# First batch's scan with two components in slices of four, VectorE's order written out

## Chip, core and metric

The kernel runs on one core of a Trainium2 chip. The core has TensorE (PE; its weight loads are listed as PEld), VectorE (DVE), ScalarE (ACT), GpSimd (POOL) and SyncE, whose queue (SPq) issues the DMAs. The metric is device time in microseconds, the median of several runs.

## What is computed

The inputs are q, k, v and a complex decay a = a_re + i a_im, each of 4 batches, 8 heads, 768 tokens and 48 channels. The part that matters here is the attention with a state:

```
mag = np.sqrt(a_re * a_re + a_im * a_im)
scale = np.minimum(mag, 0.999) / (mag + 1e-06)
a_re_n, a_im_n = (a_re * scale, a_im * scale)
for t in range(S):
    ar, ai = (a_re_n[:, :, t, :, None], a_im_n[:, :, t, :, None])
    new_re = ar * S_re - ai * S_im
    new_im = ar * S_im + ai * S_re
    kv = np.einsum('bhd,bhe->bhde', k[:, :, t], v[:, :, t])
    S_re, S_im = (new_re + kv, new_im)
    y[:, :, t] = np.einsum('bhd,bhde->bhe', q[:, :, t], S_re)
```

Then follow, for each batch, a two-dimensional Fourier transform (real part, added to its input), a normalisation, an MLP (384 to 1536 to 384), a token mixer (768 to 256 to 768) and a second MLP, each added to its input.

## The kernel before

Each batch's 768 tokens are cut into 8 chunks of 96. In a chunk the decays up to a token multiply up to a running product P, so q is multiplied by P and k is divided by it, and the attention inside a chunk is an ordinary masked product. P is a scan of 49 sequential steps for all chunks and heads at once: 128 partitions (64 pairs of head and chunk, run backwards and forwards from the middle of the chunk), 48 channels, on VectorE. Its result lies in PSUM (tiles `p`).

`stage1(b)` does this for batch b. Before the change, every batch uses the same code, in slices of three steps (`SL`, 16 slices and a last one of a single step):

- `st_a` loads the decays (`raw`) and q, k (`xx`) of a slice. For batch 0, slices 4 to 15 are loaded in large pieces of 12 steps (line 332), the first slices one by one (337, 343).
- `st_b`, `st_c`, `st_d`, `st_e` turn raw decays into factors: squares on ScalarE (351), their sum on GpSimd (356), logarithm, clamp and exponential on ScalarE (362 to 364), a Newton step (365, 366, 372 to 374) and the limit at 0.999 (382, 383). `A` then holds five rows for each step: the real part twice or as needed (384, 385), the imaginary part with both signs (386, 388) and, in row 2, the squared inverse magnitude (387).
- `st_f` is one step: 410 multiplies the three components of P (real, imaginary, and the squared inverse magnitude R) by rows 0 to 2 of `A`, 413 forms the cross products, 414 adds them. Line 407 caps R once in a slice.
- `st_g` multiplies q and k by P: 423 gives the first product, 424 multiplies the other operand by R (which turns a product with P into a division), 426 gives the second, and 427 and 428 store both in HBM (`kn`).
- `st_t` transposes them on TensorE (445) and ScalarE copies the result to `qkt` (448, 450, 451).
- `st_end` compares R times the squared length of P with 1 in the last step; `good` becomes `gate`, and a gate of zero in any batch makes a slow exact loop run at the end of the kernel (`fallback`).

After the scan, `ch_load` reads the stored products back for each chunk (`Kn`, 502), `ch_sc` forms scores (511, 518) and `ch_u`, `ch_y` carry the state from chunk to chunk (526 to 568). Beside that, `tick` and `convert` turn the 64-bit weights into pairs of 32-bit ones (181 to 203) in the background. From there on the MLPs of one batch run on TensorE while the next batch's scan runs on VectorE; for batch 0 there is no earlier batch, and the scan runs alone.

A scheduler sets the order of each engine's instructions from the program's order, priorities (`RANK`) and its own estimate of durations; each engine then runs its queue in order and waits on semaphores. `warm` adds matmuls whose result is not used (305), in batch 0 two of them from slice 10 on.

## Time and profile before

| | us |
|---|---|
| median of 3 runs | 1112.63 (1111.71, 1112.63, 1117.65) |
| the profiled execution | 1115.16 |
| its span, first to last instruction | 1113.4 |
| busy in the span: PE, DVE, ACT, POOL | 991.1, 795.6, 517.8, 372.7 |

The profiled execution is 1.8 us longer than its span, and 2.53 us above the median. The shares of busy time are averages over stages with different limits: the first batch's scan, where TensorE has little to do, its chunks with the conversion of the weights beside them, and the long stage in which TensorE multiplies.

### The profile page before, as it was taken

What the parts mean: (1) busy time and instruction counts of PE and PEld (TensorE: products, weight loads), DVE (VectorE), ACT (ScalarE), POOL (GpSimd) and SP (SyncE); (2) the same over time, 40 slices, a digit from 0 to 9 for tenths busy, and PEclk for the clock granted to TensorE, in tenths of its full rate; (3) what the DMA queues carried; (4) which work ended last, traced back from release to release, by engine and by line L of the source; (5) the groups of instructions that cost most, each with busy time, mean ns of one, the idle gap of its engine ahead of it and who ended that gap; (6) DMA issues with size and microseconds to landing.
All of it is one profiled execution on the core that took longest, in us unless ns stands there. A gap on an engine that the chain in (4) does not pass through costs nothing.

```text
span 1113.4 us, 21166 instructions
## 1 busy us (share of the span) xinstructions
PE 991.1 (89%) x7322; PEld 924.0 (83%) x7322; DVE 795.6 (71%) x2161; ACT 517.8 (47%) x1442; POOL 372.7 (33%) x510
## 2 busy tenths in 40 slices
...
GB/s 215 41 38 137 255 265 142 177 273 235 199 190 242 213 170 190 56 202 148 175 199 184 102 99 190 191 171 149 122 79 43 158 127 115 170 142 135 163 100 74
DMA packets 102466, 174.67 MB, mean 157 GB/s; under 512 B 11216, under 2 KB 63568, under 8 KB 101840
## 3 DMA queue, kind: packets, MB, share of 16 engines
...
q14 instruction: 54, 0.44, 0.1%
...
## 4 chain that ended last, share of the span: by engine, by line
PE 64%; DVE 8%; DMA 3%; ACT 1%; POOL 1%; issue 1%; SPq 0%; POOLq 0%; DVEq 0%; ACTq 0%
PE l L744 23%; PE l L728 22%; PE s L511 3%; PE s L445 2%; DMA cvt<-wL 2%; PE s L835 2%; PE s L560 2%; PE s L824 1%; PE s L566 1%; PE s L949 1%; DVE ws L784 1%; DVE ws L790 1%; PE s L526 1%; PE s L967 1%; PE s L708 1%
## 5 line engine op out<-in xcount | busy, mean ns | idle before, releaser
L744 PE MATMUL l<-w,h 128*128 128x384 f32 x1728 | 331.0, 344 | 12.8 <-DVE h L734 8.8
L728 PE MATMUL l<-th,w 128*128 128x384 f32 x1152 | 313.8, 342 | 5.3 <-DVE h L734 2.6
L744 PEld LDWEIGHTS l<-w,h 128*128 128x128 f32 x1728 | 302.8, 191 | 17.8 <-DVE h L734 12.4
L728 PEld LDWEIGHTS l<-th,w 128*128 128x128 f32 x1152 | 210.3, 189 | 9.4 <-DVE h L734 4.4
L732 ACT ACTIVATE h<-l 128x384 fp32r<-128x384 f32 x192 | 94.1, 490 | 226.0 <-PE l L728 225.2
L728 PE MATMUL l<-tl,w 128*128 128x384 f32 x576 | 194.8, 338 | 0.0
L734 DVE SCALAR_TENSOR_TENSOR h<-l,h 128x384 fp32r<-128x384 f32 x192 | 106.1, 552 | 87.9 <-ACT h L732 87.4
L747 DVE TENSOR_TENSOR u<-u,l 128x384 f32<-128x384 f32 x192 | 105.4, 550 | 76.5 <-PE l L744 75.4
L445 PE MATMUL s<-misc,y 128*112 128x128 f32 x384 | 71.0, 306 | 60.0 <-DVE y L423 38.3
L445 PEld LDWEIGHTS s<-misc,y 128*112 128x112 f32 x384 | 50.2, 148 | 77.1 <-POOL A L384 17.6
L728 PEld LDWEIGHTS l<-tl,w 128*128 128x128 f32 x576 | 108.8, 189 | 0.7 <-DVE tl L712 0.5
L192 POOL TENSOR_TENSOR cvt<-cvt 128x384 int32<-128x384 int32 x56 | 64.4, 1156 | 37.5 <-ACT sq L351 8.1
L366 POOL TENSOR_TENSOR tm<-tm 128x144 f32<-128x144 f32 (+1 forms) x68 | 35.3, 519 | 101.1 <-ACT tm L365 100.9
L511 PE MATMUL s<-qkt 112*96 112x96 f32 x512 | 59.9, 267 | 7.4 <-DVE sc L518 6.7
L511 PEld LDWEIGHTS s<-qkt 112*96 112x96 f32 x512 | 53.6, 177 | 10.6 <-DVE sc L518 7.5
L410 DVE TENSOR_TENSOR p<-p,A 128x144 f32<-128x144 f32 x192 | 59.5, 310 | 3.0
L202 POOL TENSOR_TENSOR w<-cvt,w 128x384 fp32r<-128x384 f32 x44 | 52.6, 1204 | 8.9 <-ACT w L201 8.7
L544 POOL TENSOR_TENSOR yc<-Aa,gm 48x384 f32<-48x384 f32 x18 | 21.0, 1165 | 101.4 <-DVE Aa L537 101.4
L384 POOL TENSOR_TENSOR A<-raw,tm 128x144 f32<-128x144 f32 (+1 forms) x68 | 34.9, 513 | 59.2 <-DVE tm L382 33.2
L195 DVE SCALAR_TENSOR_TENSOR cvt<-cvt 128x384 int32<-128x384 int32 x56 | 46.8, 843 | 8.7 <-POOL cvt L192 8.5
L414 DVE TENSOR_TENSOR p<-p,yt 128x96 f32<-128x96 f32 x192 | 50.1, 261 | 3.5
L934 POOL TENSOR_TENSOR xl<-u,xh 128x384 fp32r<-128x384 f32 x18 | 18.0, 1009 | 101.1 <-ACT xh L933 101.1
(182 smaller groups left out, 1805.1 us busy)
## 6 DMA issues: line engine op xcount, KB each, us to landing
...
kn<-y SPq DMA_DIRECT2D x128, 96.0 KB, 2.1
Kn<-kn SPq DMA_DIRECT2D x64, 192.0 KB, 3.9
...
```

The source lines that it names most:

```text
L192: x = ge.tensor_tensor(out=a, in0=a, in1=lo, op=ALU.add)
L195: rest(ve.scalar_tensor_tensor(out=a, in0=hi, scalar=-0x80000000, in1=a, op0=ALU.bitwise_and, op1=ALU.bitwise_or))
L202: ge.tensor_tensor(out=parts[:, 1, :], in0=a.bitcast(F32), in1=r32(parts[:, 0, :]), op=ALU.subtract)
L410: x = ve.tensor_tensor(out=cur, in0=prev, in1=A[:, j, 0:3, :], op=ALU.mult)
L414: ve.tensor_tensor(out=cur[:, 0:2, :], in0=cur[:, 0:2, :], in1=y, op=ALU.add)
L445: te.transpose(ps[:, j, :], y[:, j, 0:112], ident)
L511: te.matmul(out=ps[:, j, :], lhsT=K[:, hc, :], rhs=Q[:, hc, :])
L728: te.matmul(out=ps, lhsT=w1[:, wi, kt * 128:kt * 128 + 128], rhs=x[g][:, kt, :], start=(n == 0), stop=(n == 8))
L732: x = se.activation(out=hi, in_=ps, func=ACTF.Relu)
L734: ve.scalar_tensor_tensor(out=h[:, 1, g * 384:g * 384 + 384], in0=ps, scalar=0.0, in1=r32(hi), op0=ALU.max, op1=ALU.subtract)
L744: te.matmul(out=ps, lhsT=hs[m][:, hi, tt * 128:tt * 128 + 128], rhs=w2[:, wi, :], start=(n == 0), stop=(n == 8))
L747: ve.tensor_tensor(out=u[tt], in0=u[tt], in1=ps, op=ALU.add)
```

## The change

Batch 0 gets a scan of its own, `first_scan`; the other batches run the code as it was, now under the name `scan`. In `first_scan`:

- A slice has four steps (`SL4`, 12 slices and the last step); the two pieces of P (real and imaginary) are all that the scan carries. `A` has three rows. The clamp (363) and the second factor (374, 383, 387) are gone, and so is the cap (407).
- The inverse squared length is formed for a whole slice after its four steps (`st_s`): squares on ScalarE out of PSUM (430), sum on GpSimd (432), logarithm and exponential on ScalarE (433, 434), a product on GpSimd (435), and a Newton step on VectorE (`st_r`, 450). `st_x` (455) multiplies it into `xx`; `st_y` (444) gives the two products, `kn` is stored from 446.
- VectorE's instructions are chained by hand with `vq`: each one's place behind the one before is fixed. `line_up(i)` says which instructions of other slices stand between the three of a step. ScalarE also sums 1/|a|^2 into `low` (373), which the check at the end reads.
- All loads are issued ahead (slices 0, 1, 2 one by one, then three large pieces). `warm` starts at slice 8 of 12, two matmuls of 512 columns instead of 384.

```
-W0, WS, W1, W3 = 2, 10, 0, 0
+N4 = 4
+SL4 = [(N4 * i, N4) for i in range(12)] + [(48, 1)]
+W0, WS = 2, 8
-    ybuf = [[pool.tile([128, NT, 128], F32, name=f"y{k}{j}") for j in range(2)] for k in range(2)]
+    ybuf = [[pool.tile([128, N4, 128], F32, name=f"y{k}{j}") for j in range(2)] for k in range(2)]
...
+        def vq(x):
+            if last[0] is not None:
+                after(x, last[0])
+            last[0] = x
+            return x
...
+        def st_c(i):
+            tm = t[i]["tm"]
+            x, r0, tt = (tm[:, j, :] for j in range(3))
+            se.activation(out=r0, in_=x, func=ACTF.Ln, bias=tiny)
+            se.activation(out=r0, in_=r0, func=ACTF.Exp, scale=-0.5)
+            se.activation(out=tt, in_=r0, func=ACTF.Square, accum_out=low[:, i:i + 1])
+            ge.tensor_tensor(out=tt, in0=x, in1=tt, op=ALU.mult)
+        def st_d(i):
+            tm = t[i]["tm"]
+            r, tt = tm[:, 1, :], tm[:, 2, :]
+            vq(ve.scalar_tensor_tensor(out=r, in0=tt, scalar=-3.0, in1=r, op0=ALU.add, op1=ALU.mult))
+            se.activation(out=tt, in_=r, func=ACTF.Copy, scale=-0.25e-6 * ACL, bias=-0.5 * ACL)
+        def st_e1(i):
...
+            vq(ve.scalar_tensor_tensor(out=c1, in0=r, scalar=-2.0 / ACL, in1=tt, op0=ALU.max, op1=ALU.mult))
+            ge.tensor_tensor(out=A[:, :, 0, :], in0=raw[:, :, 0, :], in1=c1, op=ALU.mult)
+        def st_e2(i):
...
+            vq(ve.scalar_tensor_tensor(out=A[:, :, 2, :], in0=raw[:, :, 1, :], scalar=sgn, in1=d["c1"], op0=ALU.mult, op1=ALU.mult))
+            ge.tensor_scalar(out=A[:, :, 1, :], in0=A[:, :, 2, :], scalar1=-1.0, scalar2=None, op0=ALU.mult)
+            P = palloc("l" if i % 3 == 2 else "p", [128, N4, 96])
...
+            x = vq(ve.tensor_tensor(out=cur, in0=prev, in1=A[:, j, 0:1, :].to_broadcast([128, 2, 48]), op=ALU.mult))
+            marked(x)
+            d.setdefault("scan", x)
+            vq(ve.tensor_tensor(out=y, in0=prev[:, 1::-1, :], in1=A[:, j, 1:3, :], op=ALU.mult))
+            for f in between[0:1]:
+                f()
+            vq(ve.tensor_tensor(out=cur, in0=cur, in1=y, op=ALU.add))
+            for f in between[1:]:
+                f()
+        def st_s(i):
...
+            se.activation(out=e, in_=d["P"], func=ACTF.Square)
+            x, r = e[:, :, 0, :], e[:, :, 1, :]
+            ge.tensor_tensor(out=x, in0=x, in1=r, op=ALU.add)
+            se.activation(out=r, in_=x, func=ACTF.Ln, bias=wee)
+            se.activation(out=r, in_=r, func=ACTF.Exp, scale=-1.0)
+            ge.tensor_tensor(out=x, in0=x, in1=r, op=ALU.mult)
+        def st_y(i, k):
...
+            vq(ve.tensor_tensor(out=o, in0=x, in1=d["P"], op=ALU.mult))
+            h = slice(64 * k, 64 * k + 64)
+            sp.dma_start(out=knd[k, :, s0:s0 + m, :], in_=y[h, 0:m, :])
+        def st_r(i):
+            e = t[i]["ss"]
+            vq(ve.scalar_tensor_tensor(out=e[:, :, 0, :], in0=e[:, :, 0, :], scalar=-2.0, in1=e[:, :, 1, :], op0=ALU.add, op1=ALU.mult))
+        def st_x(i):
...
+            vq(ve.scalar_tensor_tensor(out=x, in0=d["ss"][:, :, 0, :], scalar=-1.0, in1=x, op0=ALU.mult, op1=ALU.mult))
...
+        def line_up(i):
+            fs = [[] for _ in range(8)]
+            if 1 < i:
+                fs[0] += [lambda: st_y(i - 2, 1), lambda: st_t(i - 2, 1)]
+            if 0 < i < NS:
+                fs[2] += [lambda: st_y(i - 1, 0), lambda: st_t(i - 1, 0)]
+                fs[6] += [lambda: st_r(i - 1)]
+                fs[7] += [lambda: st_x(i - 1)]
+            if i + 2 < NS:
+                fs[1] += [lambda: st_d(i + 2)]
+                fs[4] += [lambda: st_e1(i + 2)]
+                fs[5] += [lambda: st_e2(i + 2)]
+            return [lambda f=f: [g() for g in f] for f in fs]
...
+        if b == 0:
+            first_scan(t, knd, qk)
+        else:
+            scan(b, t, knd, qk)
```

On VectorE in the middle of batch 0's scan, before (`p` is P in PSUM, `yt` the cross products, `tm` and `A` the decays on their way to factors, `y` the products with q and k; numbers are buffers):

```order
L410 TENSOR_TENSOR p_525<-p_478,A_517 128x144
L413 TENSOR_TENSOR yt1_78<-p_478,A_517 128x96
L414 TENSOR_TENSOR p_525<-p_525,yt1_78 128x96
L407 TENSOR_SCALAR p_525<-p_525 128x48
L410 TENSOR_TENSOR p_525<-p_525,A_517 128x144
L413 TENSOR_TENSOR yt0_77<-p_525,A_517 128x96
L414 TENSOR_TENSOR p_525<-p_525,yt0_77 128x96
L410 TENSOR_TENSOR p_525<-p_525,A_517 128x144
L413 TENSOR_TENSOR yt1_78<-p_525,A_517 128x96
L414 TENSOR_TENSOR p_525<-p_525,yt1_78 128x96
L386 SCALAR_TENSOR_TENSOR A_658<-raw_181,misc_64,tm_623 128x3x48
L372 SCALAR_TENSOR_TENSOR tm_670<-tm_670 128x144
```

The same place now, the first twelve of the 19 instructions of a slice of four (`l` is P in a PSUM tile of another tag):

```order
L415 TENSOR_TENSOR l_396<-p_344,A_390 128x96
L418 TENSOR_TENSOR yt0_77<-p_344,A_390 128x96
L444 TENSOR_TENSOR y11_72<-xx_177,p_292 128x8x48
L421 TENSOR_TENSOR l_396<-l_396,yt0_77 128x96
L380 SCALAR_TENSOR_TENSOR tm_408<-tm_408 128x192
L415 TENSOR_TENSOR l_396<-l_396,A_390 128x96
L418 TENSOR_TENSOR yt1_78<-l_396,A_390 128x96
L444 TENSOR_TENSOR y00_69<-xx_177,p_344 128x8x48
L421 TENSOR_TENSOR l_396<-l_396,yt1_78 128x96
L415 TENSOR_TENSOR l_396<-l_396,A_390 128x96
L418 TENSOR_TENSOR yt0_77<-l_396,A_390 128x96
L388 SCALAR_TENSOR_TENSOR tm_408<-tm_408 128x192
```

Before, the steps stood next to each other and the rest of the slice behind them; now an instruction of another slice stands between 418 and 421 of every step, and behind 421 of three of the four.

On GpSimd in the same stage, one slice before:

```order
L366 TENSOR_TENSOR tm_435<-tm_435 128x144
L384 TENSOR_TENSOR A_376<-raw_177,tm_339 128x3x48
L374 TENSOR_SCALAR tm_435<-tm_435 128x144
L356 TENSOR_TENSOR tm_482<-sq_483 128x144
L366 TENSOR_TENSOR tm_482<-tm_482 128x144
```

and now (`ss` holds the squared length of P and its inverse):

```order
L432 TENSOR_TENSOR ss_350<-ss_350 128x4x48
L364 TENSOR_TENSOR tm_408<-tm_408 128x192
L435 TENSOR_TENSOR ss_350<-ss_350 128x4x48
L374 TENSOR_TENSOR tm_408<-tm_408 128x192
L389 TENSOR_TENSOR A_390<-raw_175,tm_304 128x4x48
L396 TENSOR_SCALAR A_390<-A_390 128x4x48
L432 TENSOR_TENSOR ss_402<-ss_402 128x4x48
```

Four instructions of 144 elements for three steps became six of 192 for four steps, in an order that ties the squared length of one slice to the factors of later ones.

On SyncE's queue where the scan ends, before (`cvt` are weights to be converted):

```order
L427 DMA kn0_99<-y01_70 64x384
L181 DMA cvt_989<-wL 128x768
L428 DMA kn0_99<-y11_72 64x384
L502 DMA Kn_1035<-kn0_99 48x8x128
L502 DMA Kn_1040<-kn0_99 48x8x128
L181 DMA cvt_993<-wL 128x768
L502 DMA Kn_1035<-kn0_99 48x8x128
L502 DMA Kn_1040<-kn0_99 48x8x128
```

and now:

```order
L446 DMA kn0_101<-y00_69 64x512
L185 DMA cvt_860<-wL 128x768
L185 DMA cvt_864<-wL 128x768
L446 DMA kn0_101<-y10_71 64x512
L446 DMA kn0_101<-y01_70 64x512
L446 DMA kn0_101<-y11_72 64x512
L744 DMA Kn_895<-kn0_101 48x8x128
L744 DMA Kn_900<-kn0_101 48x8x128
L744 DMA Kn_895<-kn0_101 48x8x128
L744 DMA Kn_900<-kn0_101 48x8x128
```

Two loads of weights moved ahead of the last three stores of `kn`, and none stands among the first loads of `Kn` any more.

## Rows read from the trace of the kernel before

**Rows 1.** Timeline of VectorE in one slice: start us, us, engine, line, operation
```profile
33.55 0.30 DVE L410 TENSOR_TENSOR p<-p,A 128x144 f32<-128x144 f32 x1
33.77 0.24 DVE L413 TENSOR_TENSOR yt<-p,A 128x96 f32<-128x96 f32 x1
...
34.95 0.26 DVE L413 TENSOR_TENSOR yt<-p,A 128x96 f32<-128x96 f32 x1
35.24 0.27 DVE L414 TENSOR_TENSOR p<-p,yt 128x96 f32<-128x96 f32 x1
35.54 0.32 DVE L410 TENSOR_TENSOR p<-p,A 128x144 f32<-128x144 f32 x1
...
36.18 0.27 DVE L414 TENSOR_TENSOR p<-p,yt 128x96 f32<-128x96 f32 x1
36.36 0.43 DVE L386 SCALAR_TENSOR_TENSOR A<-raw,misc,tm 128x144 f32<-128x144 f32 x1
36.71 0.59 DVE L372 SCALAR_TENSOR_TENSOR tm<-tm 128x144 f32<-128x144 f32 x1
37.22 0.44 DVE L423 TENSOR_TENSOR y<-xx,p 128x288 f32<-128x288 f32 x1
```
**Rows 2.** Busy time in that slice: PE, PEld, DVE, ACT, POOL, PEclk, DMA share, GB/s
```profile
33.55:38.60 5.05, 1.72 (x7) 0.95 (x6) 4.78 (x18) 3.78 (x12) 1.86 (x5) 1.00 0.16 39
```
**Rows 3.** Timeline of GpSimd in that slice
```profile
36.58 0.55 POOL L384 TENSOR_TENSOR A<-raw,tm 128x144 f32<-128x144 f32 x1
```
**Rows 4.** Where the scan starts, ends, and the chunks begin (timelines)
```profile
14.49 0.30 DVE L410 TENSOR_TENSOR p<-p,A 128x144 f32<-128x144 f32 x1
...
91.23 0.45 DVE L426 TENSOR_TENSOR y<-xx,p 128x288 f32<-128x288 f32 x1 [0.44 <-PE s L445]
...
101.90 0.34 PE L526 MATMUL l<-V,Kn 96*64 96x48 f32 x1 [2.31 <-DMA Kn<-kn]
...
108.26 1.15 POOL L545 TENSOR_TENSOR yc<-Aa,gm 48x384 f32<-48x384 f32 x1 [30.03 <-DVE Aa L537]
```
**Rows 5.** GpSimd's groups in the scan: count, busy us, mean ns, idle before
```profile
L384 POOL TENSOR_TENSOR A<-raw,tm 128x144 f32<-128x144 f32 x14 | 7.4, 526 | 2.7 <-DVE tm L382 1.6 <-DVE yt L413 0.8
L374 POOL TENSOR_SCALAR tm<-tm 128x144 f32<-128x144 f32 x14 | 4.5, 324 | 5.8 <-DVE tm L372 5.7
L384 POOL TENSOR_TENSOR A<-raw,tm 128x48 f32<-128x48 f32 x1 | 0.3, 287 | 0.5 <-DVE tm L382 0.5
```
**Rows 6.** ScalarE's groups in the scan
```profile
L448 ACT COPY qkt<-s 112x384 f32<-112x384 f32 x14 | 7.6, 540 | 6.0 <-PE s L445 5.9
L351 ACT ACTIVATE sq<-raw 128x288 f32<-128x288 f32 x12 | 5.1, 429 | 0.0
L362 ACT ACTIVATE tm<-tm,lnc 128x144 f32<-128x144 f32 x12 | 4.9, 411 | 0.8 <-POOL tm L356 0.8
L451 ACT COPY qkt<-s 112x192 f32<-112x192 f32 x13 | 4.5, 346 | 0.0
```
**Rows 7.** DMAs issued at 4.99, 91.78, 95.03 and 103.89: KB, us to landing
```profile
raw<-aL SPq DMA_DIRECT2D x1, 576.0 KB, 6.1
...
kn<-y SPq DMA_DIRECT2D x1, 96.0 KB, 3.2
...
Kn<-kn SPq DMA_DIRECT2D x1, 192.0 KB, 6.8
...
Kn<-kn SPq DMA_DIRECT2D x1, 192.0 KB, 3.3
```
**Rows 8.** TensorE's warming matmuls and transposes late in the scan
```profile
82.49 0.86 PE L445 MATMUL s<-misc,y 128*112 128x128 f32 x3 [1.32 <-DVE y L423]
83.14 2.77 PE L305 MATMUL l<-y,misc 128*128 128x384 f32 x4
```
**Rows 9.** Busy time in the chunks: columns as in rows 2
```profile
124.00:144.00 20.00, 15.83 (x182) 14.47 (x184) 17.17 (x29) 7.33 (x15) 19.69 (x14) 0.67 0.86 261
```

More of the change, by code (lines that the diff above doesn't have):

```diff
@@ L41 @@
 HOLD = mybir.DependencyInfo(mybir.DependencyClass.NoSync, mybir.DependencyReason.SCHED_ONLY)
+CHK_A, CHK_E = 6.0e4, 1.0e-7
 CHK_B, CHK_C, R_CAP = 1.5e-9, 1.0e18, 1.0e24
@@ L133, in attn_fft_mixer_kernel @@
     xT = pool.tile([112, 4, S], F32, name="xT")
-    chk = pool.tile([128, 2], F32, name="chk")
-    lnc = pool.tile([128, 4], F32, name="lnc")
-    tiny, shift, top, eps = (lnc[:, j:j + 1] for j in range(4))
+    chk = pool.tile([128, 3], F32, name="chk")
+    low = pool.tile([128, len(SL4)], F32, name="low")
+    lnc = pool.tile([128, 5], F32, name="lnc")
+    tiny, shift, top, eps, wee = (lnc[:, j:j + 1] for j in range(5))
     ve.memset(eps, 1e-6)
+    ve.memset(wee, 1e-30)
     ve.memset(tiny, 1e-18)
@@ L323, in st_a, with scan @@
+    def scan(b, t, knd, qk):
         def st_a(i):
@@ L348, in st_b @@
             n = d["n"]
-            tm = alloc(first("tmp", TT), [128, 4, 192], name="tm")[:, :, 0:n * 48]
+            tm = alloc("tmp", [128, 4, 192], name="tm")[:, :, 0:n * 48]
             sq = alloc("e", [128, n, 2, 48], name="sq")
@@ L353, in st_b @@
                 after(x, LAST[0])
-            if b == 0 and i >= AH:
-                after(x, t[i - AH]["scan"])
             ge.tensor_tensor(out=tm[:, 0, :].rearrange("p (a c) -> p a c", c=48), in0=sq[:, :, 0, :], in1=sq[:, :, 1, :], op=ALU.add)
@@ L409, in st_f @@
             y = ytmp[s % 2]
-            x = ve.tensor_tensor(out=cur, in0=prev, in1=A[:, j, 0:3, :], op=ALU.mult)
-            marked(x)
-            d.setdefault("scan", x)
+            ve.tensor_tensor(out=cur, in0=prev, in1=A[:, j, 0:3, :], op=ALU.mult)
             ve.tensor_tensor(out=y, in0=prev[:, 1::-1, :], in1=A[:, j, 3:5, :], op=ALU.mult)
```

235 lines of the change are left out of this document (169 added, 66 removed).

## The prediction

> **What bounds the kernel now.** I read the busy time by stretches first, for the stages; then the timeline of one slice of the first batch's scan, for what VectorE pays for each instruction; then the groups of GpSimd and ScalarE in the scan; last the timeline and the DMA landings around the scan's end, for what a shorter scan hands on.
>
> In the slice that starts at 33.55 us VectorE is busy 4.78 of 5.05 us, ScalarE 3.78, GpSimd 1.86 and TensorE 1.72 [rows 2]. So VectorE alone sets the pace: three steps in 5.05 us, 1.68 a step. The first step starts at 14.49 and the last product with P (426) ends at 91.23 + 0.45 = 91.68, after 77.2 us [rows 4]. Nothing of the chunks runs before that: TensorE's first matmul of a chunk waits until 101.90 for `Kn`, and GpSimd stands idle for 30.03 us until 108.26 [rows 4]. The first batch has no dense work beside it, so the scan lies on the path whole, and a microsecond off it should come off the end. Afterwards GpSimd is the busiest, 19.69 of 20 us in one stretch [rows 9], with conversions that its queue holds behind the first chunk; they move along with it.
>
> **One slice of four on VectorE.** What an instruction costs is the distance to the next start, not its duration. An instruction of 144 elements followed by one that need not wait costs 0.22 (33.55 to 33.77), 0.08 less than its 0.30. 48 elements make 0.06 (0.30 against 0.24, 0.32 against 0.26). Where the next one waits for the result, it costs 0.29 (413) or 0.30 (414); 414 followed by a stranger costs 0.18 (36.18 to 36.36) [rows 1]. From these, the 19 instructions of a slice now:
>
> - 415, 96 wide: 0.22 - 0.06 = 0.16 in the slice's first step, and 0.29 in the other three, where 418 still waits for it: 1.03.
> - 418, four times, a stranger behind it each time: 4 x 0.16 = 0.64.
> - 421, three times with a stranger behind it and once without: 3 x 0.18 + 0.30 = 0.84.
> - The two products `y` of 384: 423's 0.44 [rows 1] less 0.08 is 0.36 for 288; 96 more make 0.48: 0.96.
> - Five scalar_tensor_tensor of 192 (380, 388, 395, 450, 455): 0.22 + 0.06 = 0.28 each: 1.40.
>
> That is 4.87 for four steps, 1.22 a step instead of 1.68. It comes from 48 of 144 elements gone in 410, the cap (407) gone, 17 instructions for three steps turned into 19 for four, and waits between 413 and 414 that other slices' work now covers.
>
> **What comes on top.** In the slice before, 386 costs 0.35 (36.36 to 36.71) and 372 0.51 (36.71 to 37.22), both with a bare 0.22; together 0.42 is lost [rows 1]. Both read two tensors in SBUF, and 384 runs on GpSimd from 36.58 to 37.13 [rows 3]. Instructions that read P in PSUM keep their 0.30 to 0.32. All five in the list above are of the kind that stretches, and GpSimd has more to do: five tensor_tensor of 192 at 526 + 48 x (526 - 287)/96 = 645 ns and a tensor_scalar at some 0.38 (between 374's 0.324 and that in proportion) make 3.6 us [rows 5], 64% of the slice against 1.86/5.05 = 37%. With the loss by instructions alone it is 0.42 x 5/4 = 0.53; by elements and by GpSimd's share too, 0.42 x 5/4 x 1.33 x 1.73 = 1.21. I take 0.75, nearer the lower end because 415, 418, 421 and the products lie between the five and pass beside GpSimd. So 5.6 us a slice, with 5.4 to 6.1 for both ends.
>
> The Trainium skill (SBUF — State Buffer, "Who interferes with whom") calls this port an exclusive lock: a VectorE instruction with two SBUF inputs waits out the whole GpSimd instruction. By 384's end at 37.13, 372 would then end at 37.43; it ended at 37.30, so the trace shows something milder. With the lock and arrivals at random, each of the five would wait 0.64 x 0.3 = 0.2, 1.0 in all, and the scan would be 2 us longer than I say. Its worst alignment is a rival below.
>
> **The second bound.** ScalarE loses Relu, three ways of filling `A`, and wins three passes of `st_s`. By its groups [rows 6], in proportion: 384 wide 0.53 twice, four logarithms and exponentials of 192 at 0.46, two more passes at 0.36, the copies out of PSUM 0.68 and twice 0.43: 5.2 us of durations and about 0.2 for reading out the sum (no row shows that; 0 to 0.4). Starts overlap by 0.08, eleven times: 4.5 of 5.6. But its queue and GpSimd's are now tied into a ring: 432, 433, 434, 370, 381, 371, 471, 472, 373, 374, 389, 396 and the next 432, in that order: 3.6 less 364 and 435 is 2.3 on GpSimd, and 2.9 on ScalarE with overlaps. 5.2 is therefore the floor of a slice, and with 5.6 the ring is not late. If it slips by 0.5, VectorE waits at 415 for `A`.
>
> **Start, tail and hand-over.** The first step: slice 3's decays, once a small load, are now in the first large piece. In before that piece lands 6.1 us after its issue at 4.99, at 11.1 [rows 7], with the same bytes ahead of it, and ScalarE's square of it stands before the copies that start P. I expect the first step at 13.9 (12.5 if the piece were early, 15.0 if it lands a microsecond late). Slice 0, three steps: 3.5. Slices 1 to 9: 50.4. Slices 10 and 11, with little or nothing to prepare: 4.5 each, 9.0. Tail: after slice 11 its squared length runs through 430, 432, 433, 434, 435 (0.5 + 0.65 + 0.46 + 0.46 + 0.65 and 0.4 of hops), then 450, 455 and 444: 4.1. The last product ends at 13.9 + 3.5 + 50.4 + 9.0 + 4.1 = 80.9 instead of 91.7: 10.8 us earlier. The tail is what the new division costs: before, 426 ended even ahead of the last step.
>
> Hand-over: 10.2 us from 91.68 to 101.90 [rows 4]: the store lands after 3.2, `Kn`, issued at 95.03, after 6.8, where one that goes alone takes 3.3 [rows 7]. SyncE's queue no longer has a load of weights among the first `Kn`, so I take 5.3 for it: 0.1 + 3.2 + 5.3 = 8.6, a gain of 1.6 (0 to 3.5). Warming matmuls of 512 columns take 2.77 x 512/384 = 3.7 us for a pair at the pace of 83.14, and two groups of four transposes 2 x 0.86 x 4/3 = 2.3 [rows 8]; together 6.0, more than a slice while TensorE goes at that pace, so ScalarE's copies can be late once: 0.4 (0 to 2).
>
> **Sum.** 10.8 + 1.6 - 0.4 = 12.0 us. Against the profiled execution's 1115.16 that is 1103.2; its time stands 2.5 above the median of 1112.63, so 1100.6 on the median. I say 1100.5.
>
> **Rivals.**
>
> - *VectorE runs nearly bare* and the ring sets 5.2 a slice, `Kn` lands in 3.3: 9 x 0.4 = 3.6 and 2.0 more, and 1.4 at the start: 1093.5. For it: instructions on PSUM don't stretch [rows 1]. Against: GpSimd is busy nearly twice as much.
> - *The gain is half lost in the chunks.* If the stage from 102 on were paced by the conversions and their DMAs at their own time, an earlier start would help only in part: 1106.5. For it: 19.69 of 20 us on GpSimd and a DMA share of 0.86 at a granted clock of 0.67 [rows 9]. Against: GpSimd's idle 30 us [rows 4] show that nothing of it begins before the chunks do.
> - *The port makes it slower.* GpSimd's 389 is released by 388 and starts just as 395 comes; 450 and 455 come as 435 ends and 374 begins. If each of the five waits for a whole GpSimd instruction (3.6/6 = 0.6), a slice takes 4.87 + 3.0 = 7.9, and nine of them cost 20.5 us more than I count: 1121. It decides from 6.9 a slice (12 us over nine). Against: 372 was not held that long [rows 1].
> - *It doesn't do what it says.* The order of VectorE's queue is the one written, and the other batches' queues are nearly as they were, so I give this nothing of its own; if the new check failed, the exact loop would run and the time would be out of all proportion.
>
> **Chances.** Forecast 0.61 (its own range 1095 to 1107), nearly bare 0.14, half lost 0.15, the port 0.10. A difference under 0.5% (5.6 us, below 1107.1 or above 1118.2) can't be told from none. Faster: 0.59 of the forecast, 0.14, and 0.09 of the half lost: 0.82. Same: 0.02 + 0.06 + 0.05 of the port's milder forms: 0.13. Slower: 0.05. The range of 8 in 10 runs from 1091 to 1109.
>
> **What the profile after would show.** Right: from one slice's first 415 to the next 5.4 to 6.1 us in the middle of the scan; 418, 421 at 0.25 to 0.27 and the five others between 0.35 and 0.65; the first step near 14, the last 444 ending near 81, the first 526 near 89.5, and from there on the old distances. Wrong: 415 idle for `A` (the ring), 450 idle for GpSimd (the squared length is late), a slice over 6.9 (the port), or 526 near 90 with an end that is not earlier (lost behind it).

## The result, and the profile after

| | before | after |
|---|---|---|
| median of nine runs each | 1113.84 us | 1103.48 us |
| span of the profiled execution | 1113.4 us | 1101.6 us |
| first step (415; before 410) starts | 14.49 | 13.93 |
| last product with P (444; before 426) ends | 91.68 | 82.44 |
| first `Kn` matmul (768; before 526) starts | 101.90 | 88.75 |
| first chunk's `xT` (810; before 568) starts | 105.20 | 96.19 |
| eighth chunk's `xT` starts | 152.81 | 143.96 |
| first MLP matmul (926; before 728) starts | 195.8 | 186.2 |

The ratio of after to before is 0.9911, 95% interval 0.9893 to 0.9929: 9.9 us faster (7.9 to 11.9; 10.4 between the two medians), where 12.1 was forecast. One run of 1156.27 us stands far off the other eight (1101.60 to 1106.22); without it the median moves by 0.03.

The timeline of VectorE in one slice of the changed kernel, from its first 415 to the next slice's (start us, duration, engine, line, operation, and in brackets idle time before it and what ended it); it answers to [rows 1]:

```profile
35.09 0.27 DVE L415 TENSOR_TENSOR p<-p,A 128x96 f32<-128x96 f32 x1 [0.30 <-ACT ss L430]
...
36.06 0.43 DVE L380 SCALAR_TENSOR_TENSOR tm<-tm 128x192 f32<-128x192 f32 x1
36.41 0.25 DVE L415 TENSOR_TENSOR p<-p,A 128x96 f32<-128x96 f32 x1
...
38.54 0.75 DVE L395 SCALAR_TENSOR_TENSOR A<-raw,misc,tm 128x192 f32<-128x192 f32 x1
39.21 0.25 DVE L415 TENSOR_TENSOR p<-p,A 128x96 f32<-128x96 f32 x1
39.50 0.26 DVE L418 TENSOR_TENSOR yt<-p,A 128x96 f32<-128x96 f32 x1
39.67 0.35 DVE L450 SCALAR_TENSOR_TENSOR ss<-ss 128x192 f32<-128x192 f32 x1
39.94 0.26 DVE L421 TENSOR_TENSOR p<-p,yt 128x96 f32<-128x96 f32 x1
40.10 0.35 DVE L455 SCALAR_TENSOR_TENSOR xx<-ss,xx 128x192 f32<-128x192 f32 x1
40.75 0.27 DVE L415 TENSOR_TENSOR l<-p,A 128x96 f32<-128x96 f32 x1 [0.30 <-ACT ss L430]
```

Four steps take 40.75 - 35.09 = 5.66 us. Two places cost much more than the bare distance: 395 holds its place for 0.67 (38.54 to 39.21), 0.40 over the 0.27 that 450 takes, and 455 for 0.65, because the next 415 waits until ScalarE's 430 is done at 40.23 + 0.49 = 40.72 (timeline of ScalarE):

```profile
40.23 0.49 ACT L430 ACTIVATE ss<-p 128x384 f32<-128x384 f32 x1 [0.97 <-DVE p L421]
```

ScalarE had stood idle for 0.97 before that 430, so it was not late with other work. The same slice by engines, answering to [rows 2] (columns as there):

```profile
35.09:40.75 5.66, 2.15 (x8) 1.38 (x8) 5.22 (x19) 4.03 (x13) 3.81 (x6) 1.00 0.20 46
```

GpSimd's timeline in that slice, answering to [rows 3]:

```profile
38.49 0.59 POOL L374 TENSOR_TENSOR tm<-tm 128x192 f32<-128x192 f32 x1 [1.14 <-ACT tm L373]
39.03 0.70 POOL L389 TENSOR_TENSOR A<-raw,tm 128x192 f32<-128x192 f32 x1
39.71 0.86 POOL L396 TENSOR_SCALAR A<-A 128x192 f32<-128x192 f32 x1
```

395 (38.54 to 39.29) starts 0.05 behind 374 and ends 0.21 behind 374's end. 450 starts 0.04 ahead of 396 and keeps its 0.35, and 396 takes 0.86; 455 comes when 396 has run for 0.39, and keeps 0.35 too. GpSimd's groups over the scan (count, busy us, mean ns, idle before), answering to [rows 5]:

```profile
L396 POOL TENSOR_SCALAR A<-A 128x192 f32<-128x192 f32 x11 | 8.8, 801 | 1.2 <-DVE A L395 1.2
L374 POOL TENSOR_TENSOR tm<-tm 128x192 f32<-128x192 f32 x9 | 5.3, 587 | 7.5 <-ACT tm L373 7.5
```

396 takes 0.80 in the mean, where I had reckoned 0.38. The waits of VectorE from 14 to 82 us (who waited for whom: total us, times, longest):

```profile
DVE p L415 <- ACT ss L430: 2.1, 7, 0.3
DVE l L415 <- ACT ss L430: 1.2, 4, 0.3
DVE ss L450 <- POOL ss L435: 0.8, 1, 0.8
DVE p L415 <- POOL tm L374: 0.6, 1, 0.6
```

The wait for 430 comes back in every slice; the other two are the tail's and slice 0's.

Where the scan ends and the chunks begin, from the timelines; this answers to [rows 4]:

```profile
81.88 0.56 DVE L444 TENSOR_TENSOR y<-xx,l 128x384 f32<-128x384 f32 x1
...
88.75 0.31 PE L768 MATMUL l<-V,Kn 96*64 96x48 f32 x1 [1.48 <-DMA Kn<-kn]
...
89.95 1.60 PE L753 MATMUL s<-qkt 112*96 112x96 f32 x8
...
92.29 2.88 PE L753 MATMUL s<-qkt 112*96 112x96 f32 x16
95.10 1.04 PE L802 MATMUL l<-sc,V 96*64 96x96 f32 x16
...
96.19 0.58 ACT L810 ACTIVATE xT<-l,gate 112x384 f32<-112x384 f32 x1 [9.73 <-DVE sc L760]
```

The second half of the first chunk's scores (753 at 89.95) stands behind matmuls that wait for `Kn`, and all scores of the second chunk (92.29) stand before the first chunk's 802. Before, the timeline of TensorE had 560, the same product, right behind 526:

```profile
103.43 0.39 PE L560 MATMUL l<-sc,V 96*48 96x96 f32 x1
```

So from the first `Kn` matmul (101.90 in [rows 4]) to the first `xT` it was 3.3 us and is now 7.4. Later in the chunks the stretch that answers to [rows 9] shows GpSimd as full as it was:

```profile
124.00:144.00 20.00, 14.88 (x186) 13.53 (x186) 18.45 (x27) 7.50 (x17) 19.69 (x16) 0.86 0.93 311
```

The conversions moved along, as the forecast had it: GpSimd starts the first at 99.11 instead of 109.48 and the fortieth at 189.92 instead of 199.74.

### The profile page after: what moved, and what is told of

Read it like the earlier page. It is cut to its first block, busy times and chain, and to the rows that moved or that the text cites. A ratio compares the mean times of both kernels' runs of the same rounds, so it can differ in the third digit from the quotient of the medians.

```text
span 1101.6 us, 21033 instructions
## 1 busy us (share of the span) xinstructions
PE 985.5 (89%) x7314; PEld 923.1 (84%) x7314; DVE 784.3 (71%) x2115; ACT 506.2 (46%) x1393; POOL 387.3 (35%) x520
## 4 chain that ended last, share of the span: by engine, by line
PE 65%; DVE 10%; DMA 2%; ACT 1%; issue 1%; POOL 1%; SPq 0%; POOLq 0%; DVEq 0%; ACTq 0%
PE l L942 24%; PE l L926 22%; PE s L753 3%; PE s L642 2%; PE s L1033 2%; PE s L1022 2%; PE s L802 2%; DMA cvt<-wL 2%; PE s L808 1%; PE s L1147 1%; DVE ws L982 1%; PE s L1165 1%; PE s L768 1%; DVE cvt L199 1%; PE s L906 1%
## 5 line engine op out<-in xcount | busy, mean ns | idle before, releaser
L942 PE MATMUL l<-w,h 128*128 128x384 f32 x1728 | 332.5, 345 | 12.1 <-DVE h L932 8.4
L466 PE MATMUL s<-misc,y 128*112 128x128 f32 x96 | 22.1, 377 | 52.1 <-DVE y L444 48.6
L466 PEld LDWEIGHTS s<-misc,y 128*112 128x112 f32 x96 | 14.5, 181 | 61.9 <-issue 27.3
L753 PEld LDWEIGHTS s<-qkt 112*96 112x96 f32 x512 | 53.4, 177 | 11.1 <-DVE sc L760 8.7
L571 POOL TENSOR_TENSOR tm<-tm 128x144 f32<-128x144 f32 (+1 forms) x51 | 26.6, 523 | 73.7 <-ACT tm L570 73.7
L642 PE MATMUL s<-misc,y 128*112 128x128 f32 x288 | 45.7, 275 | 1.5 <-DVE y L626 1.0
L615 DVE TENSOR_TENSOR p<-p,A 128x144 f32<-128x144 f32 x144 | 44.7, 310 | 2.0
L589 POOL TENSOR_TENSOR A<-raw,tm 128x144 f32<-128x144 f32 (+1 forms) x51 | 26.1, 513 | 56.0 <-DVE tm L587 29.4
```

The source lines that it names most:

```text
L466: te.transpose(ps[:, j, :], y[:, j, 0:112], ident)
L615: ve.tensor_tensor(out=cur, in0=prev, in1=A[:, j, 0:3, :], op=ALU.mult)
L642: te.transpose(ps[:, j, :], y[:, j, 0:112], ident)
L753: te.matmul(out=ps[:, j, :], lhsT=K[:, hc, :], rhs=Q[:, hc, :])
L942: te.matmul(out=ps, lhsT=hs[m][:, hi, tt * 128:tt * 128 + 128], rhs=w2[:, wi, :], start=(n == 0), stop=(n == 8))
```

## The experiments

Eleven kernels, each timed in five rounds. "Scan" is the time from the first 415 to the end of the last 444, "pitch" the distance of two slices' first 415, "behind" the span less the start of the first MLP matmul. "Same" goes through TensorE's 6360 matmuls from that one on in order of time, and says how many have the same tiles and shape as the matmul at the same place of the changed kernel. The ratio is against executions of the kernel before in the same session; their medians were 1114.2 (free_order to slices_of_three), 1112.4 (factors_early to late_and_early), 1113.3 (later_order, shifted) and 1112.8 (shifted_tail), so medians of different sessions compare only to some 2 us.

| kernel | median us | ratio to before (95%) | scan | pitch | first 810 | first 926 | behind | same |
|---|---|---|---|---|---|---|---|---|
| before | 1113.8 | 1 | 77.2 | - | 105.2 | 195.8 | 917.6 | 6320 |
| after | 1103.5 | 0.9911 (0.9893-0.9929) | 68.5 | 5.66 | 96.2 | 186.2 | 915.4 | 6360 |
| free_order | 1113.9 | 1.0004 (0.9987-1.0020) | 72.6 | varies | 97.1 | 191.8 | 920.8 | 3969 |
| cover_430 | 1110.7 | 0.9965 (0.9949-0.9980) | 67.2 | 5.60 | 93.3 | 183.5 | 923.3 | 4158 |
| scores_first | 1102.0 | 0.9890 (0.9865-0.9915) | 68.5 | 5.66 | 93.7 | 183.4 | 914.1 | 6358 |
| slices_of_three | 1101.0 | 0.9883 (0.9858-0.9909) | 69.8 | 4.40 | 94.0 | 182.8 | 916.0 | 6300 |
| factors_early | 1098.4 | 0.9878 (0.9857-0.9899) | 66.4 | 5.41 | 91.7 | 180.7 | 915.8 | 6358 |
| square_late | 1115.7 | 1.0030 (1.0016-1.0044) | 72.3 | 6.00 | 97.5 | 192.2 | 921.1 | 3969 |
| reordered | 1108.3 | 0.9961 (0.9945-0.9976) | 68.8 | 5.62 | 92.4 | 183.7 | 921.4 | 3969 |
| late_and_early | 1095.1 | 0.9840 (0.9818-0.9862) | 67.2 | 5.44 | 88.9 | 181.3 | 912.5 | 6324 |
| later_order | 1111.3 | 0.9989 (0.9974-1.0004) | 66.4 | 5.41 | 88.6 | 185.4 | 924.3 | 4173 |
| shifted | 1099.5 | 0.9858 (0.9838-0.9877) | 67.2 | 5.13 | 89.8 | 181.6 | 916.8 | 6348 |
| shifted_tail | 1094.8 | 0.9853 (0.9825-0.9880) | 63.5 | 5.13 | 87.4 | 179.5 | 913.3 | 6296 |

### The written order taken away: free_order

```
         def vq(x):
-            if last[0] is not None:
+            if False:
                 after(x, last[0])
```

> The changed kernel, but without the written order: VectorE's instructions of the first scan stand as the scheduler puts them. In the middle of the scan its order differs in one thing: 388 stands behind the second step's 421 and 395 between 418 and 421 of the third step, each one place earlier. Theory (395 pays 0.40 us because it runs beside GpSimd's 374 and 389): 395 takes 0.35 to 0.45 instead of 0.75, the pitch of a slice falls from 5.66 to 5.3 to 5.4, the 0.30 that the first 415 waits for ScalarE's 430 stays, and the end comes 2 to 3 us before the changed kernel's 1103.5. Rival 1 (the written order is what makes the slice short): pitch over 6.2, the end 5 us or more later. Rival 2 (the stretch only moves to another instruction): another of the five takes over 0.6, the pitch stays 5.6 to 5.7 and the end within 1 us.

My expectation was wrong: the scheduler's order is another than I had put it. Two strangers (instructions of other slices) come to stand between 415 and 418 and two more before 421, all on the path of the steps, and 380 waits for GpSimd (VectorE's timeline):

```profile
51.07 0.26 DVE L415 TENSOR_TENSOR p<-p,A 128x96 f32<-128x96 f32 x1
51.63 0.36 DVE L380 SCALAR_TENSOR_TENSOR tm<-tm 128x192 f32<-128x192 f32 x1 [0.30 <-POOL tm L374]
51.91 0.35 DVE L455 SCALAR_TENSOR_TENSOR xx<-ss,xx 128x192 f32<-128x192 f32 x1
52.18 0.25 DVE L418 TENSOR_TENSOR yt<-p,A 128x96 f32<-128x96 f32 x1
52.35 0.56 DVE L444 TENSOR_TENSOR y<-xx,l 128x384 f32<-128x384 f32 x1
52.82 0.35 DVE L388 SCALAR_TENSOR_TENSOR tm<-tm 128x192 f32<-128x192 f32 x1
53.09 0.26 DVE L421 TENSOR_TENSOR p<-p,yt 128x96 f32<-128x96 f32 x1
```

The pitch varies from 5.0 to 7.0. The scan is 4.1 us longer; as its first step came 2.3 earlier (11.66), it ends only 1.9 later. Yet the whole gain of the change is gone: 5.6 us are lost by the first MLP matmul and 5.4 more behind it, where the same program has got another order. That raised a question that the runs below settle.

### Work put over 430: cover_430

```
-                fs[2] += [lambda: st_y(i - 1, 0), lambda: st_t(i - 1, 0)]
-                fs[7] += [lambda: st_x(i - 1)]
+                fs[7] += [lambda: st_x(i - 1)]
+                fs[7] += [lambda: st_y(i - 1, 0), lambda: st_t(i - 1, 0)]
-                fs[1] += [lambda: st_d(i + 2)]
+                fs[2] += [lambda: st_d(i + 2)]
```

> The changed kernel with the product y(i-1, 0) moved from the second step of a slice to its end, behind 455, and 380 moved into its place, so that VectorE has 0.46 us of work while ScalarE's 430 reads P. Theory (the 0.30 us idle before each slice's first 415 is on the path): that idle time falls under 0.05, one step without a stranger costs 0.12 more, the pitch goes from 5.66 to about 5.4, and the last 444 ends some 2.5 us before 82.4. In the order of TensorE's queue all eight scores of the first chunk then stand ahead of the first 768 as well, which by the theory of the scores run is worth 3 to 4 us more, so 1096 to 1099 in all. Rival (the ring of ScalarE and GpSimd sets the pace, and the wait for 430 only shows where VectorE meets it): the idle time turns up at another instruction, as a wait for A, for 381 or for 435, and the pitch stays at 5.6 to 5.7.

The wait for 430 went, and another came: 388 waits for ScalarE's 381, which came later because 380 did and because 469 had moved ahead of it (the timelines of ScalarE and VectorE):

```profile
41.00 0.35 ACT L381 ACTIVATE tm<-tm 128x192 f32<-128x192 f32 x1
...
41.00 0.26 DVE L418 TENSOR_TENSOR yt<-l,A 128x96 f32<-128x96 f32 x1
41.38 0.36 DVE L388 SCALAR_TENSOR_TENSOR tm<-tm 128x192 f32<-128x192 f32 x1
```

0.38 from 418 to 388 in place of 0.17, a bare step for 0.12, and 395 at 0.72: the pitch is 5.60. The rival was right that the wait only moves, as I had moved 380. The end, forecast at 1096 to 1099, is 7 us later than in the changed kernel though the first MLP matmul is 2.7 earlier. Here 380 starts 0.02 ahead of GpSimd's 435, and 435 is the one that is stretched, to 0.78 from its 0.59 (timelines of VectorE and GpSimd):

```profile
40.14 0.35 DVE L380 SCALAR_TENSOR_TENSOR tm<-tm 128x192 f32<-128x192 f32 x1
...
40.16 0.78 POOL L435 TENSOR_TENSOR ss<-ss 128x192 f32<-128x192 f32 x1 [0.47 <-ACT ss L434]
```

### Scores first: scores_first

```
-                te.matmul(out=ps[:, j, :], lhsT=K[:, hc, :], ...
+                st[c]["mm"] = te.matmul(out=ps[:, j, :], lhsT=K[:, hc, :], ...
-                te.matmul(out=ps[0:64, h, :], lhsT=d["kt"][:, h, 0:64], rhs=vv)
+                x = te.matmul(out=ps[0:64, h, :], ...); b or c or after(x, d["mm"])
```

> The changed kernel, but all eight scores (753) of the first chunk stand ahead of its first 768 in TensorE's queue; the scan is untouched. Theory (the second half of the scores, held behind 768's wait for Kn, is where 4 of the 13 us gained at the first 768 are given back): the first 810 starts at 92 to 93 instead of 96.2, the later ones 3 to 4 us earlier each, and the end comes 3 to 4 us before 1103.5, at about 1100. Rival (the chunks are paced by GpSimd's conversions and their transfers): the first 810 is earlier, the later ones less and less, and the end is within 1 us of 1103.5.

From the end of the last 444 to the first 810 it takes 12.1 us instead of 13.8. That is 1.7, not 3 to 4: the second chunk's scores still stand in between, as this timeline of TensorE shows:

```profile
87.88 0.31 PE L768 MATMUL l<-V,Kn 96*64 96x48 f32 x1
...
89.72 2.88 PE L753 MATMUL s<-qkt 112*96 112x96 f32 x16
92.53 1.13 PE L802 MATMUL l<-sc,V 96*64 96x96 f32 x16
```

The median is 1.5 us better, which the intervals don't tell apart from none. The scan is the changed kernel's to 0.01 us; only the first step comes 0.77 earlier (13.16), as the first large piece landed at 9.61 instead of 10.33, so that much in a first step is the loads' scatter.

### Slices of three: slices_of_three

```
-N4 = 4
-SL4 = [(N4 * i, N4) for i in range(12)] + [(48, 1)]
+N4 = 3
+SL4 = [(N4 * i, N4) for i in range(16)] + [(48, 1)]
```

> The changed kernel with slices of three steps in place of four (16 slices, two components, VectorE's order written out, warming from slice 11). Theory (the length of the slice spreads the ring, the wait for 430 and the fixed part of each instruction): 4.4 to 4.6 us for three steps, 1.47 to 1.53 a step against 5.66/4 = 1.41, so the scan takes 3 to 5 us longer and the end is at 1106 to 1109. Rival (all of the gain is the third component that is gone): 4.2 to 4.3 us for three steps and the end within 1 us of 1103.5.

30 steps from 23.27 to 67.22 make 1.465 us a step, against 1.415: just under the theory's range. But slice 0 and the tail are shorter, and the scan is only 1.3 us longer, not 3 to 5. (In TensorE's queue the first chunk's scores stand as in scores_first, so its end, forecast at 1106 to 1109, is to be compared with that: 1101.0 and 1102.0, the same.) So of the 8.7 us that the scan lost against before, the length of the slice gives 1.3 and the written order (free_order) 4.1; by difference some 3 are left for the third component and the work that went with it. No run takes that component away alone, so this share is not shown.

### 388 and 395 earlier: factors_early

```
-                fs[4] += [lambda: st_e1(i + 2)]
-                fs[5] += [lambda: st_e2(i + 2)]
+                fs[3] += [lambda: st_e1(i + 2)]
+                fs[4] += [lambda: st_e2(i + 2)]
```

> The scores_first kernel (pitch of a slice 5.66, 68.5 us from the first step to the end of the last 444, end 1102.0) with 388 and 395 one place earlier in the written order: behind the second step's 421, and between 418 and 421 of the third step. TensorE's queue keeps its order to the last row. Theory (395 pays 0.40 for running beside GpSimd's 374 and 389): 395 takes 0.35 to 0.45, one step without a stranger costs 0.12 more, the pitch falls to 5.35 to 5.45, the scan to some 65.8 and the end to 1099 to 1100. Rival (GpSimd's instructions only meet another of VectorE's): 450 or 455 takes over 0.6 in its place, pitch 5.6 to 5.7, end at 1102.

Nearly as the theory said: 395 takes 0.50 here (the timelines of VectorE and GpSimd), a little over its range, the pitch is 5.41, the scan 2.1 us shorter and the first MLP matmul 2.7 earlier. The median is 3.6 lower than that of scores_first, but from another session, and the ratios (0.9878 and 0.9890) don't tell the two apart.

```profile
37.42 0.50 DVE L395 SCALAR_TENSOR_TENSOR A<-raw,misc,tm 128x192 f32<-128x192 f32 x1
...
37.11 0.59 POOL L389 TENSOR_TENSOR A<-raw,tm 128x192 f32<-128x192 f32 x1 [0.59 <-DVE tm L388]
37.66 0.70 POOL L374 TENSOR_TENSOR tm<-tm 128x192 f32<-128x192 f32 x1
```

### 430 behind the next slice's reads: square_late

```
-            fs = [[] for _ in range(8)]
+            fs = [[lambda: st_s(i - 1)] if 0 < i < NS else []] + [[] for _ in range(7)]
...
-            st_s(i)
+            i == NS - 1 and st_s(i)
```

> The scores_first kernel with ScalarE's 430 put behind the next slice's first 415 and 418 in the program's order, so that VectorE needn't wait for it (430 waits for 418 instead); VectorE's order is untouched. Theory: the idle 0.30 before each slice's first 415 goes, the pitch falls from 5.66 to 5.3, the scan from 68.5 to some 65. For the end I expect the opposite sign: in this kernel the scheduler interleaves the later batches as it did for free_order, over 2700 rows of TensorE's queue differ, and by my theory that interleaving alone costs 5 to 8 us behind the first MLP matmul, so the end is at 1103 to 1107. Rival A (the ring of ScalarE and GpSimd sets the pace): the idle time turns up elsewhere, pitch 5.6. Rival B (the interleaving is worth nothing, free_order and cover_430 lost elsewhere): end at 1098 to 1099.

415 no longer waits (41.18 to 41.45 behind 455). But the squared length is now late, as rival A had it: on ScalarE 433 and 434 came behind 370, 381 and 371, and on GpSimd 435 behind 374 and 389, so 450 waits (the timelines of VectorE and GpSimd):

```profile
39.78 0.26 DVE L418 TENSOR_TENSOR yt<-p,A 128x96 f32<-128x96 f32 x1
40.60 0.49 DVE L450 SCALAR_TENSOR_TENSOR ss<-ss 128x192 f32<-128x192 f32 x1 [0.57 <-POOL ss L435]
...
39.98 0.59 POOL L435 TENSOR_TENSOR ss<-ss 128x192 f32<-128x192 f32 x1
```

450 then takes 0.49, as 396 started just ahead of it. Pitch 6.00, scan 3.8 longer, and behind the first MLP matmul 921.1; the end, 1115.7, is past the 1103 to 1107 that I expected, as the scan was to gain and lost.

### Another written order: reordered

```
...
-                fs[0] += [lambda: st_y(i - 2, 1), lambda: st_t(i - 2, 1)]
...
+                fs[5] += [lambda: st_r(i - 1)]
+                fs[6] += [lambda: st_x(i - 1)]
+                fs[7] += [lambda: st_y(i - 1, 1), lambda: st_t(i - 1, 1)]
...
+                fs[0] += [lambda: st_d(i + 2)]
+                fs[3] += [lambda: st_e1(i + 2)]
+                fs[4] += [lambda: st_e2(i + 2)]
...
```

The edit of scores_first and the last one of late_and_early (`ch_y`, below) are in it too.

> Another written order on the scores_first kernel: 380 in the first step, 388 and 395 one place earlier, 450 and 455 a step earlier, and y(i-1, 1) last in its own slice behind 455 in place of the next slice's first step, so it covers most of 430 and the last product needs one slice less; the first chunk's output products (802) stand ahead of the second chunk's scores too. In TensorE's queue the later batches stand as in square_late. Theory: 415's wait 0.1 to 0.15 in place of 0.30, 395 at 0.35 to 0.45, pitch 5.1 to 5.3, scan 63 to 65; the first 810 some 9 us behind the last 444; the end as late as the interleaving makes it, 1101 to 1105. Rival (450 and 455, now beside GpSimd's 374 and 389, pay what 395 paid): pitch 5.5 to 5.7.

No gain in the pitch (5.62), though not by the instructions that I had named: 450 and 455 stay at 0.35, and 395 pays again, since GpSimd's 389 now starts just with it (timelines of VectorE and GpSimd):

```profile
37.69 0.83 DVE L395 SCALAR_TENSOR_TENSOR A<-raw,misc,tm 128x192 f32<-128x192 f32 x1
...
37.72 0.59 POOL L389 TENSOR_TENSOR A<-raw,tm 128x192 f32<-128x192 f32 x1
```

The scan, 68.8, and the end, 1108.3, are both past what I expected.

### Four edits together: late_and_early

The edits of scores_first, factors_early and square_late, and the first chunk's output products ahead of the second chunk's scores:

```
-                ch_u(c)
+                ch_u(c); b or c or ch_y(c)
...
-            ch_y(c)
+            b == c == 0 or ch_y(c)
```

> All four together: eight scores first, the first chunk's output products (802) ahead of the second chunk's scores, 430 behind the next slice's first 418, 388 and 395 one place earlier. TensorE's queue in the later batches stands as in scores_first but for some 60 rows. Theory: 0.37 and 0.28 come off a slice, pitch 5.0 to 5.1 (the ring's floor was worked out as 5.2, and if it binds the pitch is 5.2 and the wait stands at 415 for A or at 388 for 381); scan 62 to 64; first 810 some 9 us behind the last 444 instead of 12; end 1094 to 1098. Rival (what the scan gains is eaten by the chunks' conversions): first 768 5 us earlier than in scores_first, the end less than 2 us earlier, 1100 or more.

The end is where I expected it, the scan is not: the pitch is 5.44, since 450 still waits 0.26 for 435 and then takes 0.49 beside 396, which started 0.06 ahead of it (timelines of VectorE and GpSimd), and the last 444 comes 6.6 us behind the last step:

```profile
37.75 0.49 DVE L450 SCALAR_TENSOR_TENSOR ss<-ss 128x192 f32<-128x192 f32 x1 [0.26 <-POOL ss L435]
...
37.68 0.68 POOL L396 TENSOR_SCALAR A<-A 128x192 f32<-128x192 f32 x1
```

What helped is the chunk: from the first 768 to the first 810 it now takes 2.6 us at a granted clock of 0.68, where the kernel before took 3.3 at 0.50, the lower of TensorE's two levels (1.2 GHz); 0.68 is a mean of both. At 0.9840 (0.9818 to 0.9862) it beats both kernels.

### The same scan with other later batches: later_order

The kernel of factors_early and the last edit (`ch_y`), nothing else.

> The factors_early kernel (scan 66.4 us, first MLP matmul at 180.7, 915.8 us from there to the end, end 1098.35) with one edit outside the scan: the first chunk's output products (802) stand ahead of the second chunk's scores. On all engines the order of the scan is the same to the last row; in the later batches the scheduler interleaves otherwise (over 3000 rows of TensorE's queue differ, of its 2954). Theory (the interleaving that the scheduler picks for the later batches is worth several us by itself, whatever the scan does): scan and first 768 as in factors_early within 0.5 us, first 810 about 2.5 us earlier, and behind the first MLP matmul 920 us or more in place of 915.8, so the end is at 1101 to 1106. Rival (free_order, cover_430 and square_late were slow for reasons of their own in the first batch): 914 to 917 us behind the first MLP matmul and the end at 1095 to 1098.

The scan, the first 768 (86.28 and 86.21) and even an earlier first 810 are there, and the kernel takes 13.0 us longer by the medians, 12.4 by the ratios. Of the spans' difference 4.6 arise by the first MLP matmul, 8.5 behind it. Busy time from 200 to 1000 us (columns as in rows 2), first of factors_early:

```profile
200.00:1000.00 800.00, 762.24 (x5748) 725.24 (x5747) 585.63 (x1608) 379.81 (x1055) 258.49 (x352) 0.97 0.53 162
```

and of later_order:

```profile
200.00:1000.00 800.00, 755.11 (x5694) 717.13 (x5693) 584.54 (x1607) 378.36 (x1059) 261.81 (x354) 0.97 0.53 160
```

TensorE does 7.1 us less in the same time, at the same granted clock; one of its new waits (who waited for whom, TensorE, 480 to 632 us of later_order: total, times, longest) is for a later batch's `Kn`, which factors_early does not have in that stretch:

```profile
PE s L768 <- DMA Kn<-kn: 3.2, 1, 3.2
```

So the theory holds, and more strongly than I had put it: an edit outside the later batches changes the order that the scheduler gives them, and that alone is worth several us. The `ch_y` edit itself is not what costs: late_and_early has it too, keeps its matmuls' places and lost nothing. In the table, the changed kernel and the six with 6296 or more matmuls in its places take 912.5 to 916.8 us behind the first MLP matmul (before 917.6), the five others, with 3969 to 4173, take 920.8 to 924.3.

### 450 a step later: shifted

```
...
+                fs[0] += [lambda: st_x(i - 2)]; fs[5] += [lambda: st_y(i - 2, 1), lambda: st_t(i - 2, 1)]
+                fs[7] += [lambda: st_r(i - 1)]
...
-                line_up(NS)[0]()
+                [f() for f in line_up(NS)]
```

> The late_and_early kernel (pitch 5.43, of which 450 waits 0.26 for GpSimd's 435; end 1095.1) with 450 put a step later, last in the slice, 455 into the first step of the next slice and y(i-2, 1) into the third step. TensorE's queue in the later batches stands as in scores_first but for some 30 rows. Theory (430 and 450 were the two waits left on VectorE): no instruction of VectorE waits over 0.1 us, pitch 4.95 to 5.15, first step to last 444 63.5 to 65.5 (the tail is some 0.3 longer), end 1091.5 to 1094. Rival 1 (450, now beside GpSimd's 396 and 364, pays 0.3 to 0.4): pitch 5.3 to 5.4 and the end within 1 us of 1095.1. Rival 2 (ScalarE's and GpSimd's ring binds at its 5.2): 388 waits for 381 or 415 for A, pitch 5.2.

The pitch is right, 5.13, with no wait on VectorE in the six slices from 27.66 us on; 455 pays 0.18 beside GpSimd's 364. It is also under the ring's "floor" of 5.2. But the scan is no shorter than in late_and_early (67.2, where I expected 63.5 to 65.5), and the end, 1099.5, is past my 1091.5 to 1094: the last 444 comes 6.9 us behind the last step. ScalarE's timeline says why:

```profile
77.24 0.54 ACT L191 ACTIVATE cvt<-cvt 128x384 f32<-128x384 f32 x1 [1.59 <-DMA cvt<-wL]
...
78.12 0.35 ACT L434 ACTIVATE ss<-ss 128x192 f32<-128x192 f32 x1
```

The last full slice's 434 stands behind a conversion that waits for its weights.

### That conversion held back: shifted_tail

```
-            se.activation(out=w[:, 0, 0, :], ... accum_out=chk[:, 0:1])
+            sq[0] = se.activation(out=w[:, 0, 0, :], ... accum_out=chk[:, 0:1])
...
+        x = se.activation(out=a.bitcast(F32), ...); sq[0] is None or after(x, sq[0])
+        x = se.activation(out=lo, ...); sq[0] is None or after(x, sq[0])
```

> The shifted kernel (pitch 5.13; but 6.9 us from the last step's 415 to the last 444, 3.2 in the changed kernel; end 1099.5) with the first conversions' activations (191, 192) held on ScalarE until behind 481, so that 434 of the last full slice no longer stands behind a conversion that waits for its weights. TensorE's queue in the later batches stands as in scores_first but for some 100 rows. Theory (the tail's 3.7 us are that one wait in ScalarE's queue): 434 starts without the 1.59 us of idle, the tail takes 3.2 to 4.0, the last 444 ends 77 to 78, the first 768 and the first 810 come 2.5 to 3.5 us earlier than in shifted, and the end is at 1095 to 1098. Rival (the transfers of kn and the half granted clock behind the scan set the hand-over): last 444 earlier, first 768 less than 1 us earlier, end at 1099 to 1100.

The scan is 3.7 us shorter (the tail 4.4, a little over the range), the first 768 and 810 come 2.4 earlier, so both parts of the theory hold but for a third of the tail's gain that the hand-over gives back (768 now waits 1.66 for `Kn`). The median is 4.7 us better and just under the range; the ratios, 0.9858 and 0.9853, don't tell the two kernels apart. With late_and_early it is the fastest here, 18.0 us under before in the medians, 16.4 by the ratio.

## Why the prediction was right, and where it was not

The time was 9.9 us under before, the forecast 12.1, in its range and on its side. By its own steps:

- **First step 13.9**: 13.93, but by another way, so that I hit it is luck. The large piece landed at 10.33, not 11.1, and ScalarE's copies were done at 11.67; then VectorE's 388, 395 and 380, which I had not listed, stood ahead of the first 415 from 12.09 on. Kernels with the same loads had the step between 11.7 (free_order) and 13.9.
- **Pitch 5.6**: 5.66, from two errors that cancel. The bare sum of 4.87 was good: 5.66 - 0.40 - 0.08 - 0.38 = 4.80. The term for GpSimd, 0.75, was too large: it costs 0.40 at 395, whose 0.75 lies outside the 0.35 to 0.65 that I had named, and 0.08 at 380. And a wait was missing, 0.38 behind 455: 415 and ScalarE's 430 both read P, and the program makes one wait for the other. I had listed 430 for its duration and not asked who reads the same tile. cover_430 and square_late took that wait away, by work put over it and by the order of the two readers. The Trainium skill (PSUM — Partial Sum Buffer, "PSUM bank collisions raise a hardware error") says that accesses of two engines to one bank must be kept apart by a semaphore, reads against reads included; by that rule the wait was to be foreseen, and the trace agrees: 3.3 us in 11 waits.
- **Why GpSimd cost less**: what decides is which of the two starts first, and I had scaled the loss by counts. Where one of the five starts behind a GpSimd tensor_tensor of 192, it ends 0.80 us after that one's start, 0.21 behind its end: 395 took 0.75 where it came 0.05 later, 0.50 where it came 0.31 later (factors_early), and 380 took 0.43 where it came 0.37 later. Where it starts first it keeps 0.35, and GpSimd's instruction is stretched: 435 to 0.78 by 380 (cover_430), 396 to 0.86 by 450, where it takes 0.68 with no such instruction just ahead of it (late_and_early). So three of the five paid nothing. One of the five doesn't fit: 395 started 0.03 to 0.04 ahead of 389 in reordered and in one slice of free_order, and still took 0.83 and 0.85. It alone takes its scalar from a tile; no run shows whether that is why. The Trainium skill (SBUF — State Buffer, "Who interferes with whom") names as partner any GpSimd instruction that reads SBUF, and says that the order of issue decides who blocks. The rows agree, on 396 too, which has one input: 450 took 0.49 where 396 had started 0.06 ahead of it. My reading of the rows before, that 372 shows something milder than a lock, was wrong in this: I had let the whole instruction run behind the other's end, while here a bare 0.35 ends 0.21 behind it (39.29 for 395, with 374 done at 39.08).
- **Slice 0, and slices 10 and 11**: 4.22 (forecast 3.5) and 9.66 (9.0); the first includes a wait of 0.6 of 415 for GpSimd's 374. The tail took 3.8 (4.1). The last product ended at 82.4 instead of 80.9.
- **Hand-over 8.6**: 6.3. The last store landed in 2.2 us, and the `Kn` issued behind it, for which 768 waited, in 3.9 (against the 3.2 and 6.8 of [rows 7]; 5.3 was forecast). So the first 768 came at 88.75; 89.5 was forecast.
- **"From there on the old distances"**: this step failed. 4.1 of the 13.2 us gained were given back by the first 810, in TensorE's order: half the first chunk's scores behind the wait for `Kn` (1.6, by scores_first), and the second chunk's scores ahead of the first's products (5.8 us from 768 to 810 there, 3.3 at a granted clock of 0.50 in shifted, where the products stand first, and 2.6 at 0.68 in late_and_early: some 2.6 by the order, the rest by the clock). The eighth chunk's `xT` was 8.85 us earlier, the first MLP matmul 9.5. How much of it reaches the end I can only bound: scores_first alone moved the median by 1.5, inside the intervals.
- **The later batches' queues are nearly as they were**: I used that sentence against a rival only; it turned out to be the condition of the whole gain. 6320 of 6360 matmuls keep their place. free_order, with 3969, has a scan 4.5 us shorter than before, and no gain; later_order shows it with the scan unchanged.
- **The rivals**: the ring did not bind (430 came after 0.97 us of idle time, and shifted, in another order, went below 5.2; the read-out of ScalarE's sum, for which I had no row, took 0.20 a slice, as I had put it). The port did not make it slower. "Half lost in the chunks" was right in kind, through an order, not through the conversions.

Open is why the last 2.2 us (behind the first MLP matmul, 917.6 to 915.4) came: kernels with almost the same order there scatter from 912.5 to 916.8, so it may be nothing.
